# A retention layer followed by a two-layer MLP on one core: GpSimd's casts and state copies given to VectorE and ScalarE, with a new order of all work

## The chip, the cores and the metric

The kernel runs on one core of a Trainium2 chip. A core has a matrix engine (TensorE, "PE" in the profile, with its weight loads shown apart as "PEld"), three engines for elementwise work (VectorE "DVE", ScalarE "ACT", GpSimd "POOL"), and a fifth, SyncE ("SP"), which here only issues DMAs. Each engine works through its own instructions strictly in order; a DMA is issued by one engine's queue and then runs on 16 shared DMA engines. The metric is the device time of one execution in microseconds, the median of several runs.

## The reference

Inputs are q, k and v, each [8 batches, 8 heads, 576 positions, 64] in float32, and two weight matrices, w_in [512, 2048] and w_out [2048, 512]. What is computed:

```python
scores = scale * np.matmul(q, k.transpose(0, 1, 3, 2))
gamma = 1.0 - 2.0 ** (-5.0 - np.arange(H))            # one decay per head
rel = pos[:, None] - pos[None, :]
Dmat = np.where(rel >= 0, gamma[:, None, None] ** rel, 0.0)
attn = np.matmul(scores * Dmat, v)                    # [8, 8, 576, 64]
x = attn.transpose(0, 2, 1, 3).reshape(4608, 512)     # tokens x (heads * 64)
h = x @ w_in
out = np.maximum(0.01 * h, h) @ w_out                 # leaky ReLU, [4608, 512] float32
```

## The kernel before

**Attention in units.** The 4608 tokens are cut into 36 units of 128 tokens (two chunks of 64). Because the decay is a power of gamma, it is split into a factor on q and a factor on the inverse side, and the sum over earlier chunks is carried from unit to unit as a state of 64 x 64 per head. Each unit u runs these jobs; their names are the words in the order below:

- `ldU.0`, `ldU.1`, `ldU.2`: loads of q, k and v of unit U, 256 KB each (line 347). Where a unit crosses from one batch to the next (unit 4, for one), a load is two DMAs. Each of the three has four buffers in turn, so the load for unit U waits for the cast of unit U-4.
- `ckU` casts k to 16 bits (line 365); `cqU` and `cvU` cast q and v and multiply them with decay factors from a table (`scaled`, lines 367 to 373). On VectorE and GpSimd a scaled cast is one instruction over 128 x 512; on ScalarE it is eight, one for each head.
- The transposes of k and q: for the first 12 units on TensorE (`tpU.1`, `tpU.0`, line 403), each followed by a copy out of PSUM (`ytU.1`, `ytU.0`, line 410); from unit 12 on by one DMA transpose on SP's queue (`trU`, line 389).
- `sbU`: TensorE forms the new part of the state (line 446). `stU.0` and `stU.1` add it to the old state on VectorE (line 480), `sgU.j` scales it at the end of a block (line 491), and `sxU` casts it to 16 bits (line 505).
- `caU`: TensorE multiplies q with the state and forms the scores (lines 543, 437); `mkU` applies the causal mask on VectorE (line 452); `owU` multiplies the scores with v (line 543); `xU` copies the result out of PSUM into x, transposed and in 16 bits (line 592).

**The MLP in groups.** Four units make a group of 512 tokens, g = 0 to 8. For groups 0 and 1 layer 1 is done plainly: `hG.F.T` is a set of matmuls (line 639), `lG.F.T` the leaky ReLU on ScalarE (line 646). From group 2 on layer 1, and for all groups layer 2, is done as a product of 2 x 2 blocks with seven instead of eight block products (the function `seven`). Layer 1 has four such sets in each group, `aG.0` to `aG.3`, layer 2 one, `bG`. In a set the parts `p1` to `p7` are the seven products on TensorE (lines 825 and 901), `cA` copies a partial sum from one PSUM bank to another (line 764), `u2` and `k5` copy partial sums to SBUF (lines 775 and 778), and `11`, `12`, `21`, `22` are the four results. `xsG.n` (line 805), `mG.n.x` (line 877), `wsN.x` (line 714) and `wmN.x` (line 685) are sums of blocks of x, of the layer's middle values, of w_in and of w_out, all on VectorE. Four PSUM banks serve the products in turn. `soG` stores output through SP's queue (line 729).

**Weights.** `wi0` to `wi3` load w_in in four pieces of 512 columns (two DMAs each, line 615), `wo0` to `wo3` load w_out in four pieces (line 621). All go through GpSimd's queue, and turn float32 into 16 bits on their way.

**What sets the order.** Three things, all written out. `CFG["loads"]` names the queue of each load. `ENGINE` lists, for each of VectorE, ScalarE and GpSimd, the jobs that it takes; a job that is not listed goes to a default (`ck`, `x`, `sx`, `cA`, `u2`, `k5` to ScalarE; `cq`, `cv`, `yt`, `sg` to VectorE). `ORDER` is one list of all jobs, some 1,440 words; an engine's own order is that list with the other engines' jobs left out. `name@n` gives the PSUM bank, and `+6@0` means six matmuls on a zero tile, whose result nobody reads. Nothing is decided while the kernel runs: an engine that comes to a job whose inputs are not there waits, with everything behind it.

The change touches `CFG`, `ENGINE` and `ORDER`, and three lines of the code. The helper that sends a job to its engine is short:

```python
ke, qe, ve = by(f"ck{u}", "ACT"), by(f"cq{u}", "DVE"), by(f"cv{u}", "DVE")
def scaled(out, x, e):
    if e != "ACT":
        engine[e].tensor_tensor(out=out, in0=t32[u, 2 * x][:], in1=decay(u, x), op=MUL)
        return
    for h in range(H):
        nc.scalar.mul(out=out[:, h, :], in_=t32[u, 2 * x][:, h, :], mul=tab_sb[:, w, x, h : h + 1])
```

## Time and profile before

| | us |
|---|---|
| median of 3 runs | 284.77 (284.27 to 285.83) |
| the profiled execution | 285.75 |
| its span, first to last instruction | 284.0 |
| busy: TensorE, its weight loads | 271.3, 230.0 |
| busy: VectorE, ScalarE, GpSimd | 234.6, 185.8, 85.5 |

A row of the groups of instructions reads: line, engine, operation, output <- inputs, shapes and types, number, then busy time and the mean duration in ns of one, then the idle time of the engine just before them and what ended it. A row of a timeline reads: start, duration, engine, line, operation, number; a bracket tells how long the engine had been idle and what it waited for. A row of the table by stretches gives, for each stretch of the span, the busy time and number of instructions of each engine. A duration is that of one instruction from its start to its end; since the next one begins before the last has quite ended, the distance from start to start is a little less. GpSimd's busy time holds its issuing of loads (line 347, 615 and 621) beside its arithmetic.

### The profile page before, as it was taken

Reading aid. Unit: us, or ns where it says so; the run is one execution under the profiler, and the core shown is the slowest. Engines: PE = TensorE matmul, PEld = TensorE weight load, DVE = VectorE, ACT = ScalarE, POOL = GpSimd, SP = SyncE. Lnnn points to the kernel's source line nnn. Section 1 sums busy time; section 2 is a strip of 40 time slices with the busy share of each in tenths; the row PEclk is TensorE's granted clock in tenths of the full one; section 3 lists DMA queues with packets and bytes.
Section 4 is the critical chain, followed back from the end, with each engine's and each line's share of the span. In section 5 each row is a group of like instructions: output and inputs, shape, how many; then the busy total and the mean of one; then the engine's idle time right before and its main releaser. Section 6 shows DMA issues by size and latency. Waiting matters only on the chain.

```text
span 284.0 us, 10281 instructions
## 1 busy us (share of the span) xinstructions
PE 271.3 (96%) x4412; PEld 230.0 (81%) x4412; DVE 234.6 (83%) x422; ACT 185.8 (65%) x401; POOL 85.5 (30%) x103
## 2 busy tenths in 40 slices
PE   7779999989999999999999999999999999999994
PEld 3358887878888888888888887888888888888883
DVE  2873889868999998988999899999889977884761
ACT  2615756716835977789589855896698576646910
POOL 8996897846230802010011132410011000000000
PEclk9999999999999999999999999999999999999999
DMA  7999899998999799889527996797849323001104
GB/s 224 251 187 256 196 246 201 197 307 204 286 224 231 176 198 178 202 165 276 106 63 173 257 242 129 159 265 164 201 79 290 79 58 130 2 2 74 76 0 149
DMA packets 115021, 49.00 MB, mean 173 GB/s; under 512 B 103712, under 2 KB 108448, under 8 KB 114976
## 3 DMA queue, kind: packets, MB, share of 16 engines
q1 hardware_dynamic: 107632, 35.14, 53.2%
q0 software_dynamic: 7056, 13.11, 19.9%
q8 instruction: 34, 0.56, 0.9%
q10 hardware_dynamic: 288, 0.11, 0.2%
q14 instruction: 11, 0.09, 0.1%
HBM read 36.81 MB, written 9.44 MB: 163 GB/s over the span
## 4 chain that ended last, share of the span: by engine, by line
PE 70%; DMA 13%; POOL 8%; DVE 3%; issue 3%; ACT 2%; POOLq 0%; DVEq 0%; ACTq 0%
PE acc L901 33%; PE acc L825 31%; POOL t L347 5%; DMA w_out<-in_moe_w_out_dram 4%; PE ot L543 3%; DMA w_in<-in_moe_w_in_dram 3%; DMA t<-in_v_dram 3%; DMA t<-in_k_dram 2%; PE sc L446 2%; DMA t<-in_q_dram 1%; PE sc L437 1%; DVE w_mix L685 1%; ACT qk L373 1%; POOL w_in L615 1%; POOL w_out L621 1%
## 5 line engine op out<-in xcount | busy, mean ns | idle before, releaser
L901 PEld LDWEIGHTS <-gt 128*128 128x128 f16 x720 | 69.4, 98 | 9.5 <-issue 0.8
L901 PE MATMUL acc<-w_out,gt 128*128 128x256 f16 x432 | 53.4, 273 | 0.6 <-DMA w_out<-in_moe_w_out_dram 0.6
L825 PEld LDWEIGHTS <-w_in 128*128 128x128 f16 x448 | 42.7, 98 | 6.9 <-issue 1.1
L843 ACT ACTIVATE gt<-acc 128x512 f16<-128x512 f32 x56 | 33.5, 599 | 11.8 <-PE acc L825 11.3
L901 PE MATMUL acc<-w_mix,gt 128*128 128x256 f16 x288 | 36.4, 273 | 0.0
L825 PEld LDWEIGHTS <-w_sum 128*128 128x128 f16 x336 | 32.1, 98 | 4.2
L851 ACT ACTIVATE gt<-sum 128x512 f16<-128x512 f32 x56 | 33.9, 631 | 0.9 <-DVE sum L847 0.8
L825 PE MATMUL acc<-xT,w_in 128*128 128x256 f16 x224 | 32.8, 273 | 1.1 <-DVE osb L938 0.6
L825 PE MATMUL acc<-xs,w_sum 128*128 128x256 f16 x224 | 33.1, 273 | 0.0
L825 PE MATMUL acc<-xs,w_in 128*128 128x256 f16 x224 | 32.7, 273 | 0.0
L639 PE MATMUL acc<-xT,w_in 128*128 128x256 f16 (+1 forms) x320 | 30.9, 251 | 1.5 <-DMA w_in<-in_moe_w_in_dram 1.5
L369 POOL TENSOR_TENSOR v<-t,cs 128x512 f16<-128x512 f32 x14 | 15.7, 1120 | 55.3 <-PE ot L543 45.5
L901 PEld LDWEIGHTS <-mix 128*128 128x128 f16 x288 | 27.9, 98 | 3.9 <-issue 0.5
L452 DVE TENSOR_TENSOR s<-sc,cs 128x512 f16<-128x512 f32 x36 | 24.6, 683 | 5.3 <-PE sc L437 4.8
L639 PEld LDWEIGHTS <-w_in 128*128 128x128 f16 x320 | 25.5, 98 | 4.1 <-issue 1.9
L646 ACT ACTIVATE gt<-acc 128x512 f16<-128x512 f32 x32 | 18.0, 600 | 13.5 <-PE acc L639 13.5
L775 ACT COPY u<-acc 128x512 f32<-128x512 f32 x30 | 17.6, 586 | 13.5 <-PE acc L901 9.9
L764 ACT COPY acc<-acc 128x512 f32<-128x512 f32 x27 | 15.5, 573 | 13.8 <-PE acc L825 8.3
L847 DVE TENSOR_TENSOR sum<-acc,k 128x512 f32<-128x512 f32 x28 | 19.3, 688 | 5.7 <-PE acc L825 2.8
L847 DVE TENSOR_TENSOR sum<-acc,u 128x512 f32<-128x512 f32 x28 | 19.2, 686 | 3.8 <-PE acc L825 3.5
L369 POOL TENSOR_TENSOR qk<-t,cs 128x512 f16<-128x512 f32 x12 | 13.2, 1104 | 27.2 <-DMA t<-in_q_dram 19.2
L592 ACT CAST xT<-ot 128x512 f16<-128x512 f32 x25 | 14.6, 587 | 8.2 <-PE ot L543 7.5
(70 smaller groups left out, 491.1 us busy)
## 6 DMA issues: line engine op xcount, KB each, us to landing
out_dram<-osb SPq DMA_DIRECT2D x17, 512.0 KB, 4.0
t<-in_k_dram SPq DMA_DIRECT2D x22, 256.0 KB, 4.9
t<-in_q_dram SPq DMA_DIRECT2D x22, 256.0 KB, 4.3
t<-in_v_dram SPq DMA_DIRECT2D x21, 256.0 KB, 4.2
t<-in_v_dram POOLq DMA_DIRECT2D x11, 256.0 KB, 4.7
t<-in_q_dram POOLq DMA_DIRECT2D x10, 256.0 KB, 5.5
t<-in_k_dram POOLq DMA_DIRECT2D x10, 256.0 KB, 4.6
w_in<-in_moe_w_in_dram POOLq DMA_DIRECT2D x8, 256.0 KB, 7.1
```

The lines of the kernel that those rows point to most:

```text
L369: engine[e].tensor_tensor(out=out, in0=t32[u, 2 * x][:], in1=decay(u, x), op=MUL)
L452: landed[u] = nc.vector.tensor_tensor(out=s[:], in0=sc[:, :, 0], in1=mask_sb.unsqueeze(1).unsqueeze(1).to_broadcast([P, 2, NP, CH]), op=MUL,)
L592: copies[xe](out=x_of(u).rearrange("q c (j t) -> q j c t", j=2), in_=at)
L639: nc.tensor.matmul(out=a[:, n, :], lhsT=w_in16[:, c, (f0 + n) * P : (f0 + n + 1) * P], rhs=x[:, c, t0 : t0 + nt], start=(n == 0 and c == 0 ...
L646: nc.scalar.activation(out=y[:, f0 : f0 + nf, t0 : t0 + nt], in_=a[:], func=mybir.ActivationFunctionType.Lrelu)
L764: copies[ce](out=B[:], in_=A[:])
L775: op("u2", ue, lambda: copies[ue](out=u2[:], in_=B[:]), [done["6"]], [u2], [B])
L825: nc.tensor.matmul(out=r[:, f, :], lhsT=w[:, c, (2 * n + f) * P : (2 * n + f + 1) * P], rhs=rhs[:, c, :], start=fresh and c == 0 and f == ...
L843: w = op(what, "ACT", lambda: nc.scalar.activation(out=to(), in_=r[:], func=lr), after, [y], [r])
L847: what, "DVE", lambda: nc.vector.tensor_tensor(out=s[:], in0=r[:], in1=plus[:], op=ADD),
L851: f"l{g}.{n}.{what}", "ACT", lambda: nc.scalar.activation(out=to(), in_=s[:], func=lr), [j], [y],
L901: nc.tensor.matmul(out=(r[tb] if isinstance(r, tuple) else r)[:, tb, :], lhsT=lhs[n]()[:, f, tb * P : (tb + 1) * P], rhs=rhs[n][:, f, :], ...
```

## The change

GpSimd keeps only its DMA issues. Its fifty other jobs (14 `cv`, 12 `cq`, 9 `ck`, 7 `sg`, 8 `sx`) go to VectorE or ScalarE. Between VectorE and ScalarE themselves many jobs change places too, in both directions: copies out of PSUM, casts and results of layer 2. The load of v of unit 12 goes from SP's queue to GpSimd's. `ORDER` is new from the first line to the last, with nine instead of twelve places for the matmuls on a zero tile (27 of these instead of 28). A new setting `half` is 0 and changes nothing that is computed or how. The diff, cut to its core (lines of `loads`, the new and the old `ENGINE`, the beginning and the end of `ORDER`):

```diff
-        ("u", 12, "SP"), ("u", 13, "SP"), ("u", 14, "SP"), ("u", 15, "SP"), ("u", 16, "SP"), ("u", 17, "SP"),
...
+        ("u", 12, ("SP", "SP", "POOL")), ("u", 13, "SP"), ("u", 14, "SP"), ("u", 15, "SP"), ("u", 16, "SP"),
...
+        "DVE": """
+            ck0 cq1 cq0 yt1.0 cv0 cv1 yt0.0 ck2 cq2 cv2 cq3 x0 yt1.1 yt2.0 cv3 yt3.1 yt4.1 yt3.0 cv4 cq4 x3 cq5 sx4.1
+            cv5 cv6 ck7 cq6 x5 yt6.1 yt6.0 cq7 cv8 yt7.0 sx7 x7 cv9 sx8.0 cq8 yt8.0 cv10 cv11 b0.k5 cq11 sx9 yt9.1
+            yt9.0 yt10.1 yt10.0 sx10 cq14 cv12 yt11.1 cv13 x10 cv14 ck15 a2.0.u2 a2.1.u2 a2.2.k5 cq15 ck16 cv16
+            a2.3.u2 cq18 cq16 cq17 sx16 cv18 cq19 sx17.0 cv19 cq20 a3.2.k5 a3.2.u2 a3.3.u2 cv20 cq21 sx20 cv21 cv22
...
         "ACT": """
...
-            ck0 yt0.0 sx0 ck2 yt1.1 cv2 yt1.0 x0 yt3.0 x2 yt3.1 yt4.0 cv5 x4 yt5.0 x5 sx6 yt7.1 sx7 x6 sx8.0 yt8.0
...
+            yt0.1 ck1 sx0 ck3 ck4 sx1 sx2 yt2.1 x1 x2 sx3 yt4.0 ck5 yt5.1 x4 yt5.0 sx5 ck6 cv7 yt7.1 sx6 ck8 x6 ck9
...
-        "DVE": """
-            yt0.1 cq0 cv0 cq1 cv1 ck1 cv3 cq3 yt2.0 yt2.1 sx2 x1 sg3.1 sx3 cq4 x3 ck4 yt4.1 cv4 yt5.1 cq5 sx4.1 sx5
...
-        "POOL": """
-            cq2 sg1.1 sx1 ck3 ck5 ck7 cv7 cv8 cv9 sg8.0 ck9 cv10 sx9 cq9 sg10.1 cq11 cq10 cv13 ck13 cq15 cv14 sg12.1
-            ck17 cq17 sx13.1 cv16 cq18 cq16 cq21 cv19 cv21 sx19 cv24 cq25 sg24.0 sx24 sx25 cq29 cv27 cv28 sx27 cv29
-            ck29 sg28.1 sx28 ck30 ck32 cv34 cq35 sg35.0
...
-    ld0.1 ld0.0 ld1.0 ld0.2 ld1.2 ld1.1 ck0 +6@0 +1@1 +1@2 +1@3 tp0.1@0 ld2.1 yt0.1 ld2.2 cq0 ld2.0 +6@1 tp0.0@2 cv0
-    yt0.0 cq1 ld3.2 +1@3 sb0 cv1 tp1.0@0 ld3.0 ck1 st0.0 +2@1 tp1.1@3 ld3.1 st0.1 +1@2 sb1 sx0 wi1 ck2 ca0 yt1.1 mk0
-    tp2.1@1 cv2 cq2 st1.0 ow0 wi0 cv3 st1.1 yt1.0 cq3 +5@2 sb2 x0 sg1.1 tp3.0@3 tp2.0@2 st2.0 sx1 yt2.0 yt3.0 ck3
-    yt2.1 +2@0 ca1 st2.1 ld4.0 tp3.1@3 mk1 sx2 +1@0 ow1 sb3 ca2 wi2 h0.4.0@2 x1 ld4.1 mk2 h0.4.128@1 l0.4.0 st3.0
...
-    b8.p6.1 m8.3.0 b8.p5.1 m8.3.1 b8.u2 b8.p7.0 b8.k5 b8.p7.1 b8.p2.0 b8.22 b8.p4.0 b8.11x so8.11x b8.p4.1 b8.p3.0
-    b8.21 b8.p3.1 so8.1 b8.p2.1 b8.12 so8.12 b8.11y so8.11y
...
+    ld0.1 ld0.0 ld1.0 ld0.2 ld1.1 ld1.2 ck0 +6@0 +1@1 +1@2 tp0.1@3 ld2.1 yt0.1 ld2.0 cq1 cq0 +7@0 tp1.0@1 ld3.1 yt1.0
+    tp0.0@2 cv0 ld2.2 ck1 +1@3 sb0 ld3.0 st0.0 cv1 ld4.1 yt0.0 st0.1 ck2 +7@0 sb1 sx0 cq2 ld3.2 ca0 tp2.1@1 st1.0
+    tp1.1@3 ck3 tp2.0@2 mk0 wi1 st1.1 +1@0 ow0 cv2 tp3.1@0 wi0 sg1.1 sb2 cq3 st2.0 ck4 ld4.0 x0 sx1 st2.1 yt1.1 sx2
+    yt2.0 ld4.2 tp4.1@3 yt2.1 cv3 ca1 tp3.0@2 mk1 +1@1 ow1 sb3 ca2 x1 mk2 wi2 yt3.1 +2@1 ow2 st3.0 h0.4.128@1 yt4.1
+    st3.1 h0.4.0@0 sg3.1 l0.4.128 yt3.0 x2 l0.4.0 h0.4.256@3 sx3 ld5.0 ca3 l0.4.256 h0.0.256@1 mk3 ld5.1 ld5.2 cv4
...
+    b8.p6.1 b8.p2.0 b8.u2 b8.p7.0 b8.11x so8.11x b8.p7.1 b8.p2.1 b8.22 m8.3.1 b8.p4.0 b8.11y so8.11y b8.p4.1 b8.p3.0
+    b8.21 so8.1 b8.p3.1 b8.12 so8.12
...
-        z = Buf(xs_pool, [P, 4, 2, HT], F16, "xs", turn=g - CFG["plain1"])
+        z = Buf(xs_pool, [P, 4, 2, HT], F16, "xs", turn=g - CFG["plain1"] + CFG["half"])
```

More of the change, by code (lines that the diff above doesn't have):

```diff
@@ L68 @@
     turned=12,
+    half=0,
     order='1265734',
@@ L213 @@
+    a8.2.p4.0 a8.3.k5 a8.3.p7.0 a8.2.21 m8.0.0 a8.3.p3.0 l8.2.22 b8.p1.0@2,0 a8.3.22 l8.2.12 a8.3.12 l8.3.22 b8.p1.1
+    m8.1.0 l8.3.12 a8.3.p4.0 m8.0.1 b8.p5.0@3 a8.3.21 m8.2.1 b8.cA@1 b8.p5.1 m8.1.1 b8.p6.0 m8.2.0 b8.k5 m8.3.0
+    b8.p6.1 b8.p2.0 b8.u2 b8.p7.0 b8.11x so8.11x b8.p7.1 b8.p2.1 b8.22 m8.3.1 b8.p4.0 b8.11y so8.11y b8.p4.1 b8.p3.0
+    b8.21 so8.1 b8.p3.1 b8.12 so8.12
 """
@@ L985 @@
         for i in range(16):
-            layer1(g, 2 * (i % 8), 2, 2 * P * (i // 8), 2 * P)
+            if g + 1 < CFG["plain1"] or i % 4 < 2 or not CFG["half"]:
+                layer1(g, 2 * (i % 8), 2, 2 * P * (i // 8), 2 * P)
     mix_weights()
@@ L989 @@
     for g in range(NG):
-        if g >= CFG["plain1"]:
+        whole_plain = CFG["plain1"] - CFG["half"]
+        if g >= whole_plain:
             z = x_sums(g)
-            for n in range(HF // 2):
+            for n in range(HF // 4 if g < CFG["plain1"] else 0, HF // 2):
                 layer1_set(g, n, z)
```

209 lines of the change are left out of this document (101 added, 108 removed), and 7 rows, old and new, of the table loads.

## The prediction

> **What bounds the kernel now.** I read the head of the page, then a table of busy time by stretch, then TensorE's own timeline for the places where it waits, then the chain of work that ended last. First the head of the page and six stretches of the table (columns: stretch, length, then busy time and instructions of each engine, granted TensorE clock, DMA share, GB/s).
>
> ```profile
> PE 271.3 (96%) x4412; PEld 230.0 (81%) x4412; DVE 234.6 (83%) x422; ACT 185.8 (65%) x401; POOL 85.5 (30%) x103
> ...
> 0.00:20.00 20.00, 14.21 (x251) 7.79 (x252) 12.34 (x26) 7.76 (x18) 18.83 (x28) 1.00 0.94 222
> 40.00:60.00 20.00, 18.86 (x319) 16.16 (x320) 16.55 (x27) 11.89 (x23) 16.68 (x19) 1.00 1.09 209
> 80.00:100.00 20.00, 20.00 (x355) 16.99 (x353) 19.47 (x38) 13.11 (x25) 8.24 (x9) 1.00 0.96 199
> 260.00:284.00 24.00, 20.23 (x182) 17.43 (x179) 13.50 (x21) 9.60 (x19) 0.00 (x0) 1.00 0.18 67
> ...
> 137.60:188.10 50.50, 49.86 (x914) 42.79 (x913) 47.52 (x85) 39.14 (x89) 11.76 (x14) 1.00 0.72 166
> 20.00:260.00 240.00, 236.85 (x3986) 204.77 (x3984) 208.78 (x376) 168.45 (x365) 66.69 (x76) 1.00 0.78 179
> ```
>
> From 20 to 260 us TensorE is without work for 240.00 - 236.85 = 3.15 us, at a granted clock of 1.00. The rest of its idle time lies in the first 20 us (5.8) and in the last 24 (3.8). The same matmuls are to be done after the change, so between 20 and 260 us nothing can be won but these 3.15 us; a delay has no such limit. VectorE is full in places (19.47 of 20), GpSimd in the first 60 us. TensorE's timeline shows where the idle time lies (in brackets the idle time before the row, and what ended it):
>
> ```profile
> 19.15 1.95 PE L639 MATMUL acc<-xT,w_in 128*128 128x128 f16 x32 [1.46 <-DMA w_in<-in_moe_w_in_dram]
> ...
> 21.81 1.95 PE L639 MATMUL acc<-xT,w_in 128*128 128x128 f16 x32
> ...
> 43.25 0.38 PE L403 MATMUL acc<-ident,qk 128*128 128x128 f16 x4 [0.53 <-DVE qkT L410]
> ...
> 57.20 1.03 PE L901 MATMUL acc<-w_out,gt 128*128 128x256 f16 x8 [0.61 <-DMA w_out<-in_moe_w_out_dram]
> ...
> 62.83 0.38 PE L901 MATMUL acc<-w_mix,mix 128*128 128x256 f16 x2 [0.32 <-DVE w_mix L685]
> ...
> 72.23 0.22 PE L543 MATMUL ot<-qkT,st 64*64 64x64 f16 x2 [0.39 <-ACT qkT L410]
> ...
> 117.51 0.60 PE L825 MATMUL acc<-xT,w_in 128*128 128x256 f16 x4 [0.51 <-ACT acc L764]
> ...
> 172.96 0.60 PE L825 MATMUL acc<-xT,w_in 128*128 128x256 f16 x4 [0.62 <-DVE osb L938]
> ```
>
> Six waits after 20 us make 0.53+0.61+0.32+0.39+0.51+0.62 = 2.98 of the 3.15 us. The first layer-1 matmul waits for a piece of w_in. The chain that ended last says the same: GpSimd's issues and the transfers of w_in and w_out early on, TensorE at the end.
>
> ```profile
> 11.70 1.08 POOL qk L369
> ...
> 13.32 8.35 DMA w_in<-in_moe_w_in_dram
> ...
> 50.19 10.34 DMA w_out<-in_moe_w_out_dram
> ...
> 267.81 12.43 PE acc L901 x112
> ...
> 280.27 0.37 ACT osb L936
> ```
>
> The row at 267.81 gives TensorE's pace: 12.43 / 112 = 0.111 us for each matmul of 256 columns.
>
> **The change part by part.** *Work that moves.* Fifty jobs leave GpSimd: 14 cv, 12 cq, 9 ck, 7 sg, 8 sx. Several others change places between VectorE and ScalarE. Counted by the two tables of engines, VectorE gains 17 long and 14 short instructions net, ScalarE 17 single ones and two of the scaled casts that it does in eight parts. Prices, from the timelines of VectorE, ScalarE and GpSimd (start, duration):
>
> ```profile
> 6.16 0.69 DVE L369 TENSOR_TENSOR qk<-t,cs 128x512 f16<-128x512 f32 x1 [0.60 <-DMA t<-in_q_dram]
> 6.78 0.69 DVE L369 TENSOR_TENSOR v<-t,cs 128x512 f16<-128x512 f32 x1
> ...
> 8.59 0.42 DVE L365 CAST qk<-t 128x512 f16<-128x512 f32 x1
> 8.93 0.42 DVE L478 COPY s<-sc 128x256 f32<-128x256 f32 x1
> ...
> 113.20 1.27 DVE L491 TENSOR_TENSOR s<-stmp,cs 128x256 f32<-128x256 f32 x1
> ...
> 169.85 1.52 DVE L369 TENSOR_TENSOR v<-t,cs 128x512 f16<-128x512 f32 x1
> ...
> 172.23 0.68 DVE L938 TENSOR_TENSOR osb<-acc,u 128x512 f32<-128x512 f32 x1
> ```
> ```profile
> 11.36 2.02 ACT L373 ACTIVATE v<-t,cs 128x64 f16<-128x64 f32 x8
> 13.28 0.57 ACT L410 COPY qkT<-acc 128x512 f16<-128x512 f16 x1
> ```
> ```profile
> 8.43 1.05 POOL L347 DMA_DIRECT2D t<-in_q_dram  x1
> 9.48 0.88 POOL L347 DMA_DIRECT2D t<-in_k_dram  x1
> ...
> 15.92 1.61 POOL L347 DMA_DIRECT2D t<-in_q_dram  x2
> ...
> 29.62 0.61 POOL L365 CAST qk<-t 128x512 f16<-128x512 f32 x1 [2.90 <-PE acc L639]
> ...
> 113.09 1.10 POOL L369 TENSOR_TENSOR v<-t,cs 128x512 f16<-128x512 f32 x1 [0.77 <-DVE osb L938]
> ...
> 169.34 1.49 POOL L369 TENSOR_TENSOR v<-t,cs 128x512 f16<-128x512 f32 x1
> ```
>
> A long VectorE instruction follows the next after 6.78 - 6.16 = 0.62 us, a short one after 8.93 - 8.59 = 0.34. So VectorE gains 17 x 0.62 + 14 x 0.34 = 15.3 us; ScalarE 17 x 0.57 + 2 x 2.02 = 13.7 us, on 185.8, which leaves it at 70% of the span. ScalarE's part is hidden by its idle third; if a part of it stands ahead of a copy that frees a bank, TensorE pays it, and that is in the last term of the sum.
>
> *What VectorE gets back.* The scaled cast of v at 169.85 took 1.52 us while GpSimd ran another (169.34 to 170.83); alone it takes 0.69. The scaling at 113.20 took 1.27 beside GpSimd's of 113.09; as a short one I put it at 0.42. Each lost about 0.85 us. The groups of instructions, shapes apart (count, then busy us and mean ns), show how often:
>
> ```profile
> L369 DVE TENSOR_TENSOR v<-t,cs 128x512 f16<-128x512 f32 x16 | 14.0, 882 | 0.0
> L877 DVE TENSOR_TENSOR gt<-gt 128x1024 f16<-128x1024 f16 x18 | 13.9, 778 | 0.0
> ```
>
> Against 0.69 that is 16 x 0.19 + 18 x 0.09 = 4.7 us in these two groups. With GpSimd out of the arithmetic it goes, and VectorE's net gain is 15.3 - 4.7 = 10.6 us, to 245.2 (86% of the span). The waits at 117.51 and 172.96 stand right behind the two stretched instructions: at 172.96 TensorE waits for a VectorE sum that ran at 172.23, 0.85 us late; at 117.51 for a ScalarE copy behind VectorE's line. Both waits (0.51 and 0.62) are shorter than what is given back. I take -1.1 us; the bounds are 0 (something else is late there next) and -1.1.
>
> *w_out.* GpSimd's casts stood between its loads: the one at 29.62 held the queue 2.90 us for its data. Without them the loads go out earlier, but the DMA engines are full then (share 1.09 from 40 to 60 us). I take 2.9 us earlier, the one hold that left the queue empty; bounds 0 and 2.9 and more. The new order asks for the second piece of w_out (b0.p1.1) some 18 matmuls of 0.111 us, 2.0 us, sooner. Net 0.9 us, about what the waits of 0.61 and 0.32 need: -0.9, between -0.9 and +2.0.
>
> *The front.* In the new order k of unit 4, two DMAs of together 1.6 us of issue (as q of that unit at 15.92), goes ahead of the first w_in piece. That piece then comes 0.9 (one load's issue at 9.48) to 1.6 us later; I take 0.9, since the transfers and not the issues are the slower there (8.35 us to land). The scaled cast of 1.08 us between the two w_in pieces is gone, so the second comes -0.2 to +0.9 later. Before the change TensorE had two layer-1 steps on the first piece (19.15 for 1.95) and took up the second at 21.81, just after it landed (13.32 + 8.35 = 21.67). The new order has three such steps first, so it hardly waits for the second: of 0.9 us some 0.5 are made good, +0.4 (0 to +1.2). VectorE has 12 long and 17 short instructions ahead of that first step, 13.2 us from 6.16 on, so until 19.4; w_in comes at about 20.05. The cover is 0.6 us thin.
>
> *v of unit 12* moves from SP's queue to the end of GpSimd's, behind all its other loads. SP's queue starts with k of unit 12 instead; nothing waits behind GpSimd's last issue, and its cast comes some 18 us of matmuls later. Price 0; if the DMA engines hold it, the cast waits on VectorE with all behind it.
>
> *The end.* Before, TensorE's last product is followed by a 0.37 us copy and a store of 128 KB; now by the sum b8.12 and a store of 256 KB. The sum takes 0.69 us:
>
> ```profile
> 279.39 0.69 DVE L938 TENSOR_TENSOR osb<-acc,u 128x512 f32<-128x512 f32 x1 [1.06 <-PE acc L901]
> ...
> out_dram<-osb SPq DMA_DIRECT2D x17, 512.0 KB, 4.0
> out_dram<-osb SPq DMA_DIRECT2D x2, 128.0 KB, 1.7
> ```
>
> That is +0.3 for the sum, and for the store between 0 and (4.0 - 1.7) = 2.3; being twice the small one and half the large, I take a little over the small one, +0.2. Together +0.5.
>
> *New waits.* An order made anew has its own. Waits of the other kind in the old one (0.53 and 0.39) stay at their size. For the fuller VectorE and ScalarE I add 0.8 us, near the 0.92 of those two; the bounds are 0 and the 10.6 us by which VectorE grows.
>
> Sum: -1.1 - 0.9 + 0.4 + 0.5 + 0.8 = -0.3 us. The profiled execution took 285.75 us (its span 284.0), the median of the runs 284.77, 0.98 less. 285.75 - 0.3 - 0.98 = 284.4 us.
>
> **A rule weighed.** The issue at 8.43 took 1.05 us, while VectorE's cast of 8.59 ran, against 0.88 for the next: 0.17 us lost. Ahead of the first w_in piece the new order has two such casts on VectorE (k of units 0 and 2), the old one had one (unit 1): 0.17 us more, and the sum would be -0.1; I leave it in the front's bounds. The Trainium skill, "SBUF — State Buffer", sections "SBUF: two separate sides" and "A bandwidth-pool intuition that's wrong (but worth ruling out)", says that such a copy keeps GpSimd from writing its DMA descriptors, and gives some 3.1 us for an issue of 0.62. By that figure, an estimate, w_in would come 2.5 us later and the sum would be about +1.7 with the 0.5 made good. The direction agrees with the row, the size is fifteen times the row's, and the row decides.
>
> **The rivals.** *Slower: VectorE becomes the bound in the middle.* From a4.0.p1 to a6.0.p1 both orders have 392 matmuls; VectorE has 60 long instructions in both, and 25 short ones before, 32 after. In 50.50 us it was busy 47.52. The seven add 2.4 us, to 49.9; freedom from GpSimd's 14 jobs there gives back 0 to 14 x 0.85, at least the 0.85 of 169.85. With nothing else back, VectorE is at 49.1 of 50.5, and half its idle time of 3.0 us must go. Against: from 80 to 100 us it was busy 19.47 of 20, and TensorE did not wait. It decides when VectorE waits for data or for a product over 1.4 us in that stretch; if it waits the 3.0 as before, TensorE is 1.6 us late there, and twice that over the like stretches before and after. In place of 0.8: -0.3 - 0.8 + 3.2 + 1.2 (the front at its upper end, 0.8 more, and 0.4 for w_out) = +3.3, so 288.1 us.
>
> *Faster: the new order has no waits of its own.* Then all of the 3.15 us goes, and only the end is left: -3.15 + 0.4 + 0.5 = -2.25, 282.5 us; with the front made good too, 282.1. For it: load leads are longer (casts of units 9 to 11 come 9 to 18 us of matmuls behind their loads, 7 to 14 before). Against: fuller engines.
>
> *TensorE has room.* Its weight loads were busy 81%, and 16.99 of 20 us where matmuls had no gap at all, so 85% is full here; at 85% for the whole, 230.0 / 0.85 = 271 us. The matmul pace of 0.111 us without gaps speaks against it. The Trainium skill, "Perfetto Trace Analysis", section "Identifying the Most-Contended Engine", holds weight-load busy time to be the measure of room, and matmul busy time not.
>
> *Slower: casts hold the loads.* The one early cast more on VectorE stops GpSimd's issues for longer than the 0.17 us seen. To bring the sum from -0.3 to +1.7 it must cost 2.0 us; the time is then 284.77 + 1.7 = 286.5. The issues at 8.43 and 9.48, 1.05 and 0.88, with and without such a cast beside them, speak against it.
>
> **How the numbers follow.** Half a per cent, 1.4 us, is about what a measurement can tell from no change: 283.35 to 286.2. Forecast 0.39; VectorE bound 0.29; casts that hold the loads 0.03; no waits of its own 0.27; room on TensorE 0.02. So faster 0.29, same 0.39, slower 0.32. The forecast's own range, from the bounds of the front, the end and w_out, is 283.4 to 286.2. The range goes to 281.6, half a microsecond below the faster rival, and 288.2, the slower rival.
>
> **What would show it.** Scaled casts on VectorE at 0.69 us with no GpSimd arithmetic in the groups; no wait for w_out near 57 us; the first layer-1 matmul at about 20 us; no wait like those at 117.51 and 172.96; b8.12 last. The prediction is wrong if VectorE's line in the middle shows gaps and TensorE waits for its sums, or if ScalarE stands long before a cast (k of unit 28, on ScalarE, comes only some 4.5 us of matmuls behind its load).

## The result and the profile after

The changed kernel takes 283.32 us (median of 20 executions, 282.45 to 285.72). The kernel before, run beside it, takes 285.61 us (20 executions, 284.27 to 289.16). The ratio is 0.9927, with an interval of 0.9907 to 0.9947: it is faster by 0.7%. The 284.77 us that the prediction started from is the median of three of these twenty executions of the kernel before; that of all twenty is 0.84 us higher.

The profiled execution of the changed kernel was the slowest of its twenty, 285.72 us. So a second profile of the same kernel was taken later, of an execution of 283.01 us (median there 283.31). Both are shown; the second is the typical one. In the changed kernel the line numbers are lower by three (901 became 898, 825 became 822, 639 became 636, 369 became 366).

The head of the page and the summary of the chain that ended last, then rows of the table by stretches, first profile:

```profile
PE 273.8 (96%) x4411; PEld 232.3 (82%) x4411; DVE 237.9 (84%) x453; ACT 198.2 (70%) x434; POOL 40.9 (14%) x54
...
PE 92%; DMA 4%; POOL 2%; DVE 1%; issue 0%; POOLq 0%
...
20.00:260.00 240.00, 239.89 (x4040) 207.23 (x4032) 213.84 (x408) 180.12 (x401) 24.60 (x30) 0.99 0.78 177
138.30:188.30 50.00, 50.00 (x902) 43.02 (x899) 48.21 (x95) 39.55 (x88) 0.00 (x0) 1.00 0.87 182
```

GpSimd does nothing behind its last load issue, VectorE and ScalarE have more to do (213.84 and 180.12 us between 20 and 260, against 208.78 and 168.45 before), and TensorE's idle time in these 240 us went from 3.15 us to 0.11 (its matmuls ran at half clock in the first six of them, of which more below). In the stretch of the sets a4 to a6 (138.30 to 188.30) VectorE is busy 48.21 of 50.00 us and TensorE 50.00 of 50.00: the engine that feeds it is nearly full, and it is never late. TensorE's timeline has no row with a wait between 30 and 280 us. What there is lies in the first 30:

```profile
16.38 0.58 PE L400 MATMUL acc<-ident,qk 128*128 128x128 f16 x4 [2.21 <-DVE qkT L407]
19.52 0.43 PE L540 MATMUL ot<-s,v 64*64 64x64 f16 x16 [1.12 <-DVE s L449]
21.95 4.66 PE L636 MATMUL acc<-xT,w_in 128*128 128x128 f16 x48
...
278.23 1.91 PE L898 MATMUL acc<-w_out,gt 128*128 128x256 f16 x16
```

The same kernel's second profile, table by stretches and TensorE's timeline:

```profile
20.00:260.00 240.00, 239.32 (x4017) 206.87 (x4018) 214.71 (x409) 181.62 (x404) 23.90 (x28) 1.00 0.78 180
...
16.12 0.58 PE L400 MATMUL acc<-ident,qk 128*128 128x128 f16 x4 [2.21 <-DVE qkT L407]
20.26 1.96 PE L636 MATMUL acc<-xT,w_in 128*128 128x128 f16 x32
...
275.52 1.91 PE L898 MATMUL acc<-w_out,gt 128*128 128x256 f16 x16
```

Three points of time cut each execution into front, middle and end: the first layer-1 matmul, the end of the last matmul (start plus duration of its row; before: 277.45 + 2.78), and the end of the span. For the two profiles after, the last three columns are differences to before.

| | first layer-1 matmul | end of last matmul | end of span | front | middle | end |
|---|---|---|---|---|---|---|
| before | 19.15 | 280.23 | 284.0 | 19.15 | 261.08 | 3.8 |
| after, first profile | 21.95 | 280.14 | 283.9 | +2.80 | -2.89 | under 0.1 |
| after, second profile | 20.26 | 277.43 | 281.2 | +1.11 | -3.91 | under 0.1 |

So the new kernel starts layer 1 about 1 us later, has a middle nearly 4 us shorter, and ends as before. About 0.5 us of both is work that moved, not time lost and won. Ahead of its first layer-1 matmul the new order has a set of four transposes (k of unit 4) and the 24 matmuls of `ow2` more than the old one. Rows of TensorE's timeline, second profile, then before:

```profile
19.95 0.32 PE L540 MATMUL ot<-s,v 64*64 64x64 f16 x16
20.09 0.23 PE L540 MATMUL ot<-qkT,st 64*64 64x64 f16 x8
```
```profile
21.03 0.32 PE L543 MATMUL ot<-s,v 64*64 64x64 f16 x16
```

From 19.95 to the layer-1 matmul at 20.26 `ow2` takes 0.31 us; before, it comes behind the first layer-1 matmul, at 21.03. The four transposes add some 0.22 (eight of them last 0.62 us in the profile of before, four 0.40). At equal work the second profile therefore loses 1.11 - 0.53 = 0.58 us in front and wins 3.91 - 0.53 = 3.38 us in the middle.

Why the first profile lost more in front can be read from its rows. The chain has the load of v of unit 3; VectorE's timeline has its cast, which stands ahead of the mask of unit 1 (line 449) that TensorE is waiting for:

```profile
10.62 7.53 DMA t<-in_v_dram
...
15.91 0.75 DVE L407 COPY qkT<-acc 128x512 f16<-128x512 f16 x2
18.17 0.69 DVE L366 TENSOR_TENSOR v<-t,cs 128x512 f16<-128x512 f32 x1 [1.51 <-DMA t<-in_v_dram]
18.78 0.68 DVE L449 TENSOR_TENSOR s<-sc,cs 128x512 f16<-128x512 f32 x1
```

The load landed at 10.62 + 7.53 = 18.15 us. In the second profile the same cast ran at 16.32 us without a wait. TensorE was then idle a second time, and its granted clock stayed low; table by stretches (PE alone; the column behind its busy time is the clock), first and second profile:

```profile
18.00:20.00 2.00, 0.88 (x38) 0.50 1.24 213
20.00:22.00 2.00, 2.00 (x71) 0.50 1.07 282
22.00:24.00 2.00, 2.00 (x24) 0.50 1.08 193
```
```profile
16.00:18.00 2.00, 1.88 (x33) 0.50 1.14 165
18.00:20.00 2.00, 1.86 (x72) 0.66 1.22 217
20.00:22.00 2.00, 2.00 (x55) 1.00 1.12 296
```

The Trainium skill, "TensorE: Matmul & The Clock Gate", section "Part 1: The HAM clock gate (the "warmup" mystery)", puts the clock at half after an idle window of some 3.4 us. The half agrees (0.50); an idle time of 2.21 us, behind a stretch with shorter gaps, was enough here.

### The profile page after: what moved, and what is told of

It reads as the page before. It is cut to its first block, busy times and chain, and to the rows that moved or that the text cites. A ratio compares the mean times of both kernels' runs of the same rounds, so it can differ in the third digit from the quotient of the medians.

```text
span 283.9 us, 10247 instructions
## 1 busy us (share of the span) xinstructions
PE 273.8 (96%) x4411; PEld 232.3 (82%) x4411; DVE 237.9 (84%) x453; ACT 198.2 (70%) x434; POOL 40.9 (14%) x54
## 4 chain that ended last, share of the span: by engine, by line
PE 92%; DMA 4%; POOL 2%; DVE 1%; issue 0%; POOLq 0%
PE acc L898 40%; PE acc L822 31%; PE acc L636 11%; PE ot L540 5%; DMA t<-in_v_dram 4%; PE sc L443 2%; PE sc L434 2%; POOL t L344 2%; PE acc L400 1%; PE acc L957 0%; DVE osb L935 0%; DVE v L366 0%; DVE s L449 0%; POOLq L344 0%; POOLq L1009 0%
## 5 line engine op out<-in xcount | busy, mean ns | idle before, releaser
L898 PE MATMUL acc<-w_out,gt 128*128 128x256 f16 x432 | 54.4, 273 | 0.0
L822 PEld LDWEIGHTS <-w_in 128*128 128x128 f16 x448 | 43.1, 98 | 5.7 <-issue 0.3
L840 ACT ACTIVATE gt<-acc 128x512 f16<-128x512 f32 x56 | 33.4, 599 | 10.8 <-PE acc L822 10.6
L636 PE MATMUL acc<-xT,w_in 128*128 128x256 f16 (+1 forms) x320 | 32.2, 262 | 0.0
L636 PEld LDWEIGHTS <-w_in 128*128 128x128 f16 x320 | 27.1, 104 | 2.5 <-DVE xT L589 0.2
L761 ACT COPY acc<-acc 128x512 f32<-128x512 f32 x32 | 18.4, 574 | 13.3 <-PE acc L822 9.1
L772 ACT COPY u<-acc 128x512 f32<-128x512 f32 x26 | 15.3, 589 | 8.9 <-PE acc L898 4.5
L366 DVE TENSOR_TENSOR qk<-t,cs 128x512 f16<-128x512 f32 x29 | 19.8, 685 | 1.9 <-DMA t<-in_q_dram 1.9
L366 DVE TENSOR_TENSOR v<-t,cs 128x512 f16<-128x512 f32 x29 | 19.7, 685 | 1.6 <-DMA t<-in_v_dram 1.5
L589 ACT CAST xT<-ot 128x512 f16<-128x512 f32 x28 | 16.3, 588 | 6.7 <-PE ot L540 6.4
```

Source lines behind the costliest of these rows:

```text
L589: copies[xe](out=x_of(u).rearrange("q c (j t) -> q j c t", j=2), in_=at)
L636: nc.tensor.matmul(out=a[:, n, :], lhsT=w_in16[:, c, (f0 + n) * P : (f0 + n + 1) * P], rhs=x[:, c, t0 : t0 + nt], start=(n == 0 and c == 0 ...
L761: copies[ce](out=B[:], in_=A[:])
L772: op("u2", ue, lambda: copies[ue](out=u2[:], in_=B[:]), [done["6"]], [u2], [B])
L822: nc.tensor.matmul(out=r[:, f, :], lhsT=w[:, c, (2 * n + f) * P : (2 * n + f + 1) * P], rhs=rhs[:, c, :], start=fresh and c == 0 and f == ...
L840: w = op(what, "ACT", lambda: nc.scalar.activation(out=to(), in_=r[:], func=lr), after, [y], [r])
```

## The experiments

The prediction gave two reasons for a gain (GpSimd's arithmetic no longer stretches VectorE's; w_out comes earlier) and feared two losses (new waits, a later front). The experiments ask which part of the change does what. All ratios are against the kernel before, run in the same batch.

| run | ratio | 95% interval |
|---|---|---|
| the change | 0.9927 | 0.9907 to 0.9947 |
| the change, second time | 0.9927 | 0.9903 to 0.9951 |
| old order, three casts off GpSimd | 1.0003 | 0.9970 to 1.0036 |
| old order, twelve early jobs off GpSimd | 1.0049 | 1.0013 to 1.0086 |
| old order, all fifty jobs off GpSimd | 1.0269 | 1.0227 to 1.0311 |
| old order, whole new table of engines | 1.0696 | 1.0634 to 1.0758 |
| new order, late 33 jobs back on GpSimd | 0.9922 | 0.9889 to 0.9954 |
| new order, all fifty back on GpSimd | 1.0213 | 1.0136 to 1.0290 |
| new, nine short jobs more on VectorE | 1.0010 | 0.9975 to 1.0045 |
| new, w_in ahead of k of unit 4 | 1.0151 | 1.0126 to 1.0177 |
| new, another front | 0.9901 | 0.9875 to 0.9928 |
| new, another front, old end | 0.9902 | 0.9868 to 0.9936 |
| new, another front, late 33 back on GpSimd | 0.9905 | 0.9867 to 0.9942 |

### The old order with three casts off GpSimd

```diff
         "DVE": """
+            cv19 cv27 cv28
...
         "POOL": """
-            ... cv19 ... cv27 cv28 ...
```

> The old kernel with only three casts of v (units 19, 27 and 28) taken from GpSimd to VectorE, at their old places in the order. In the trace of before each of them ran beside a VectorE instruction that took 1.3 to 1.5 us instead of 0.42 to 0.69. Theory (collision): the TensorE waits of 0.51 us at 117.5 and 0.62 us at 173.0 go, although VectorE gets 3 x 0.62 = 1.9 us more work; the time falls by 1.1 to 1.5 us, ratio about 0.995. Rival (VectorE is simply full there): the waits stay or move, ratio 1.000 to 1.005.

Measured: ratio 1.0003. TensorE's timeline and the table by stretches of this run (lines are higher by one than before):

```profile
172.03 0.60 PE L826 MATMUL acc<-xT,w_in 128*128 128x256 f16 x4 [0.56 <-DVE osb L939]
...
100.00:120.00 20.00, 20.00 (x344) 17.27 (x342) 19.34 (x40) 15.10 (x38) 1.04 (x1) 1.00 1.04 203
```

The wait at 117.51 is gone, so there the collision was its cause, or at least enough to cause it. The wait at 172 stays, though GpSimd's cast is gone: VectorE's sum is late there anyway (VectorE is busy 19.78 of 20 us from 160 to 180 in this run). By the waits about half of the -1.1 us in the prediction was right. In time nothing of it shows: the theory's 0.995 missed, and an interval of 0.3% (0.9 us) to either side can't tell half a microsecond from none.

### The new order with the late jobs back on GpSimd

Units 12 and up: 33 jobs (the expectation says 34).

```diff
         (the same jobs go out of "DVE" and "ACT")
+        "POOL": """
+            cv13 ck13 cq15 cv14 sg12.1 ck17 cq17 sx13.1 cv16 cq18 cq16 cq21 cv19 cv21 sx19 cv24 cq25 sg24.0 sx24
+            sx25 cq29 cv27 cv28 sx27 cv29 ck29 sg28.1 sx28 ck30 ck32 cv34 cq35 sg35.0
+        """,
```

> The new kernel and its new order, but with the jobs of units 12 to 35 that GpSimd had before (34 of the 50) given back to it. It is the table alone, undone for the part behind the loads. Theory (collision): VectorE and ScalarE are less full, but VectorE's scaled casts and scalings beside GpSimd's stretch to over 1 us again, and TensorE has waits of 0.5 us and more between 60 and 240 us, 1 to 3 us in sum; ratio to the old kernel 0.996 to 1.003. Rival (the new order made the gain, and where the casts run does not matter): no more waits than in the new kernel (0.1 us), ratio 0.993.

Measured: ratio 0.9922, no different from the change. The table by stretches:

```profile
20.00:260.00 240.00, 239.66 (x4020) 207.07 (x4020) 207.45 (x387) 173.97 (x375) 55.45 (x61) 1.00 0.81 180
```

GpSimd works 55.45 us beside VectorE, and TensorE idles 0.34 us. VectorE is stretched now and then here too (a sum of 128 x 1024 of 1.10 us at 160.30, 0.93 at 168.41, instead of 0.69), but nothing waits for it at that time. Behind the loads, then, it isn't GpSimd's silence that makes TensorE's line free of waits.

### The new order with all fifty jobs back on GpSimd

This differs from the run above by the 17 jobs of units 1 to 11. The exchange of other jobs between VectorE and ScalarE stays as in the changed kernel. (The new order with the whole old table was not run, so what that exchange is worth in the new order stays open.)

> The new order and the new loads, with all fifty jobs put back on GpSimd, the twelve early ones among its load issues too. Theory (the order alone carries the gain behind the loads): between 80 and 260 us TensorE idles under 0.5 us as in the changed kernel; if the early jobs cost the loads nothing either, the ratio to before is 0.990 to 0.995. By the rival that the freed GpSimd queue is what brings w_out early, w_out lands 5 us or more later than in the changed kernel, a wait of 0.5 us or more for it stands near 50 us, the two casts of q of unit 2 and k of unit 3 hold w_in by 1 to 2 us, and the ratio is 0.997 to 1.005.

Measured: ratio 1.0213. The profiled execution, 294.30 us, is the slowest of its four (the others: 289.48 to 292.77), so the sizes below are those of one execution. Both ratios expected miss. The theory's first half holds: behind 80 us TensorE is as full as in the changed kernel (busy 20.00 us in eight of the nine stretches of 20 us from 80 to 260, and 19.97 in the other), so the loss lies ahead of that. The rival's cause is not there: w_in and w_out aren't what TensorE waits for. The timelines of VectorE, GpSimd and TensorE around the largest wait, and the table by stretches:

```profile
58.70 3.18 DVE L877 TENSOR_TENSOR gt<-gt,mix 128x1024 f16<-128x1024 f16 x1
...
59.27 1.06 POOL L369 TENSOR_TENSOR qk<-t,cs 128x512 f16<-128x512 f32 x1
60.27 1.05 POOL L369 TENSOR_TENSOR v<-t,cs 128x512 f16<-128x512 f32 x1
61.27 2.95 POOL L369 TENSOR_TENSOR qk<-t,cs 128x512 f16<-128x512 f32 x2
61.80 1.52 DVE L685 TENSOR_TENSOR w_mix<-w_out 128x1024 f16<-128x1024 f16 x1
...
63.25 1.53 DVE L877 TENSOR_TENSOR mix<-mix,gt 128x1024 f16<-128x1024 f16 x1
65.03 0.68 DVE L369 TENSOR_TENSOR qk<-t,cs 128x512 f16<-128x512 f32 x1
...
65.77 0.61 PE L403 MATMUL acc<-ident,qk 128*128 128x128 f16 x4 [3.82 <-DVE qk L369]
...
60.00:80.00 20.00, 16.18 (x170) 13.47 (x169) 16.36 (x25) 6.87 (x17) 5.96 (x7) 0.83 0.48 115
```

Four scaled casts on GpSimd, nearly back to back since its queue had been held (4.13 us, for a product of VectorE, up to 55.58), meet three sums on VectorE, which take 3.18, 1.52 and 1.53 us in place of 0.68. That is 4.2 us on VectorE's line, and the cast behind them (65.03) is what TensorE waits 3.82 us for. With the wait the granted clock falls too: 0.83 in the mean from 60 to 80 us. Here GpSimd's arithmetic is the cause, at many times the 0.85 us of the prediction. The rest of the loss lies in the first 60 us: waits that the changed kernel doesn't have, of 1.18 us at 12.99, 0.72 at 34.09, 0.65 at 43.37 and 0.38 at 50.55 (all but the second for VectorE), and a granted clock of 0.50 from 14 to 22 us.

### The old order with the twelve early jobs off GpSimd

```diff
         "DVE": """
+            cq2 sg1.1 sx1 ck3 ck5 ck7 cv7 cv8 cv9 sg8.0 ck9 cv10
```

> The kernel before with its twelve early GpSimd jobs (casts and copies of units 1 to 10, which stand among the issues of w_in, w_out and units 5 to 11) on VectorE; all else as before. By the prediction's step for w_out the waits of 0.61 (57.20 us) and 0.32 (62.83 us) go, for -0.9 us, less what VectorE's eight long and four short instructions cost the first 20 us (0 to 1 us): ratio 0.997 to 1.000. By the rival that VectorE pays at the front, as the changed kernel did, the first layer-1 matmul comes 1 to 3 us later than 19.15 and the ratio is 1.000 to 1.010.

Measured: ratio 1.0049. The first layer-1 matmul comes at 18.32 us, 0.83 earlier than before, and the waits of 0.61 and 0.32 us at 57 and 63 us are gone, as the prediction's step for w_out says. (The wait of 0.61 is not a sure sign: the run with three casts, whose first 60 us are those of the kernel before, doesn't have it either, though its last piece of w_out is issued at 49.94 us.) TensorE's timeline shows where it is lost again (lines higher by one than before):

```profile
76.08 2.06 PE L902 MATMUL acc<-w_mix,mix 128*128 128x256 f16 x16 [1.34 <-DVE mix L878]
...
173.38 0.60 PE L826 MATMUL acc<-xT,w_in 128*128 128x256 f16 x4 [1.42 <-DVE osb L939]
```

VectorE, with more ahead of a product's sum, is late for it at 76 us, and the wait at 173 is 1.42 us where it was 0.62. The rival put the loss in front; it came behind, so the rival's ratio, 1.000 to 1.010, was met by another way than it said.

### The old order with the whole new table, and with the fifty jobs alone

The first run takes the new `ENGINE` whole, the second moves only the fifty GpSimd jobs (34 to VectorE, 16 to ScalarE) and leaves the other 117 that the new table places elsewhere. `ORDER` and the loads are the old ones in both.

> The old order of issue and the old loads, with the new table of engines: GpSimd does no cast or copy any more. By the theory that the gain comes from taking arithmetic off GpSimd, the waits at 57.20, 117.51 and 172.96 us of the kernel before go and the time falls by 1 to 2 us (ratio 0.993 to 0.997). By the theory that the order made anew carries the gain, an order that was made for another table has waits of its own: TensorE idles at least the 3.15 us of before between 20 and 260 us, and the time is no lower than before, up to 3 us above (ratio 1.000 to 1.010).

> The kernel before, its order and loads unchanged, with only the fifty GpSimd jobs moved: 34 to VectorE and 16 to ScalarE, as in the new table; the other 117 jobs that the new table places elsewhere (between VectorE and ScalarE) stay where they were. If the old order's loss with the whole new table (16.9 us at TensorE's last matmul) came from those 117 jobs, this kernel is near the one before, ratio 0.997 to 1.010. If taking the work off GpSimd is what the old order cannot bear, because VectorE and ScalarE are asked for more between two products than fits, it loses most of it too: ratio 1.02 to 1.06, with TensorE waiting for VectorE and ScalarE all along the middle.

Measured: 1.0696 and 1.0269. The first is far above both of its expected ranges; the second lies in that of its second theory. Table by stretches and summary of the chain, for the whole table and then for the fifty jobs:

```profile
20.00:260.00 240.00, 225.99 (x3833) 191.66 (x3830) 201.18 (x384) 172.39 (x389) 24.13 (x29) 1.00 0.78 176
...
PE 53%; ACT 20%; DVE 15%; issue 5%; DMA 4%; SPq 1%; POOL 0%; ACTq 0%; DVEq 0%; POOLq 0%
```
```profile
20.00:260.00 240.00, 233.14 (x3924) 200.38 (x3922) 210.31 (x402) 178.47 (x413) 25.05 (x30) 0.99 0.78 177
...
PE 76%; DMA 7%; ACT 7%; DVE 6%; issue 2%; POOL 2%; SPq 0%; ACTq 0%; POOLq 0%
...
74.64 0.22 PE L545 MATMUL ot<-qkT,st 64*64 64x64 f16 x2 [1.32 <-ACT qkT L412]
...
218.87 0.60 PE L827 MATMUL acc<-xs,w_sum 128*128 128x256 f16 x4 [1.65 <-ACT u L777]
```

ScalarE's timeline ahead of that last wait, again with the fifty jobs alone:

```profile
215.85 2.02 ACT L375 ACTIVATE v<-t,cs 128x64 f16<-128x64 f32 x8
217.77 0.57 ACT L938 COPY osb<-acc 128x512 f32<-128x512 f32 x1
218.24 0.58 ACT L777 COPY u<-acc 128x512 f32<-128x512 f32 x1
```

VectorE and ScalarE do no more between 20 and 260 us than in the changed kernel (210.31 and 178.47 against 213.84 and 180.12), and yet TensorE waits 6.9 us in the one and 0.11 in the other. What differs, where the rows show it, is which job stands ahead of which: the cast of a v that came from GpSimd, 2.02 us in its eight parts, now stands on ScalarE ahead of the copy that TensorE waits for (218.24), since the order has it there. In the old order, taking the work off GpSimd is a loss of 2.7%, and the other moves of the table cost 4% more.

### More work on VectorE

```diff
         "DVE": """
+            ck21 ck22 sx19 ck23 sx21 sx23 ck25 ck26 ck28
...
         "ACT": """
-            (the same nine)
```

> The changed kernel with nine short jobs of units 19 to 28 (casts of k of units 21, 22, 23, 25, 26 and 28, state copies of units 19, 21 and 23) moved from ScalarE to VectorE: 9 x 0.34 = 3.1 us more on VectorE between 133 and 170 us, where it has 50.00 - 48.21 = 1.8 us idle in 50. By the rival that VectorE is at its limit in the middle, TensorE pays what does not fit, 3.1 - 1.3 = 1.8 us or more, in waits ended by VectorE, and the time rises by 1.5 to 3 us (ratio to before 0.998 to 1.004). By the theory that the work ahead of each product has slack in it, waits stay under 0.5 us and the ratio is that of the changed kernel, 0.990 to 0.995.

Measured: ratio 1.0010, where the changed kernel has 0.9927; in spans, 282.8 against the 281.2 of the second profile, +1.6 us. The stretch that holds the nine jobs, in this run and in the second profile of the changed kernel:

```profile
130.00:170.00 40.00, 39.06 (x691) 33.15 (x689) 39.35 (x81) 25.37 (x52) 0.00 (x0) 1.00 0.80 177
...
137.21 1.05 PE L899 MATMUL acc<-w_out,gt 128*128 128x256 f16 x8 [0.78 <-DVE gt L875]
```
```profile
130.00:170.00 40.00, 40.00 (x705) 34.40 (x702) 38.66 (x76) 31.00 (x64) 0.00 (x0) 1.00 0.85 181
```

VectorE goes from 38.66 to 39.35 of 40 us, and TensorE from full to 39.06. Of 3.1 us put on VectorE 1.6 to 2.1 come out at the end, as the rival said (1.8): VectorE is near its limit in the middle, with about 1 us of room in 40. The run can't tell, though, how much of this is VectorE's fullness and how much the places of the nine jobs, in an order that was made for them on ScalarE.

### The front

The first of two runs moves the load of k of unit 4 behind w_in. The second has the copies `yt1.1` and `x0` on ScalarE, ahead of the cast of k of unit 4, and the cast of v of unit 3 behind the mask of unit 1.

```diff
-    ... ld3.0 st0.0 cv1 ld4.1 yt0.0 ... sg1.1 sb2 cq3 st2.0 ck4 ld4.0 ...
+    ... ld3.0 st0.0 cv1 yt0.0 ... sg1.1 sb2 cq3 st2.0 ld4.1 ck4 ld4.0 ...
```
```diff
-    ... cq3 st2.0 ck4 ld4.0 x0 sx1 st2.1 yt1.1 sx2 ... yt2.1 cv3 ca1 tp3.0@2 mk1 +1@1 ow1 sb3 ca2 ...
+    ... yt1.1 x0 cq3 st2.0 ck4 ld4.0 sx1 st2.1 sx2 ... yt2.1 ca1 tp3.0@2 mk1 cv3 +1@1 ow1 ca2 sb3 ...
```

> The new kernel with one load moved: k of unit 4 (two DMAs) is issued behind the first two pieces of w_in instead of ahead of them. It undoes the step that I priced at +0.9 us of lateness and +0.4 us of time. Theory (the load ahead of w_in makes the front late): the first w_in piece is issued at 10.1 instead of 11.5 us and lands a microsecond earlier, the cast of v of unit 3 comes earlier too, and the time falls by 0.4 to 2 us; ratio 0.986 to 0.991. Rival (the front is held by VectorE's and ScalarE's lines, where the cast of k of unit 4 now comes later and holds the state casts sx1 and sx2 on ScalarE): no change or 1 us longer, ratio 0.993 to 0.997.

> The new kernel with its front loosened: the copy yt1.1 and the output copy x0 go from VectorE to ScalarE and stand before the cast of k of unit 4; on VectorE the cast of v of unit 3 stands behind the mask of unit 1 instead of before it; the state products of unit 3 stand behind the scores of unit 2. In the new kernel TensorE waited 2.2 us at 16.4 and 1.1 us at 19.5, its clock fell to about half from 14 to 27 us, and the first layer-1 step began at 21.95. Theory (VectorE's line and the late v of unit 3 hold the front): the first step begins at about 20.5, the clock stays near full, 1.5 to 3 us less than the new kernel; ratio to the old one 0.982 to 0.988. Rival (w_in's landing at 20.4 alone sets the front): the first step comes at 20.4 at the low clock, no more than 0.5 us less, ratio 0.991 to 0.993.

Measured: 1.0151 and 0.9901. With w_in first, TensorE's timeline has

```profile
22.47 0.61 PE L401 MATMUL acc<-ident,qk 128*128 128x128 f16 x4 [8.37 <-ACT qk L363]
```

ScalarE stands at the cast of k of unit 4, whose load now comes late, with the state copies of units 1 and 2 behind it; the rival named this, but allowed it 1 us. So the early load of k isn't what costs the front: the order needs it there. With the other front the wait of 2.21 us shrinks to 0.34 and the first layer-1 matmul comes at 19.80 us:

```profile
14.65 0.40 PE L402 MATMUL acc<-ident,qk 128*128 128x128 f16 x4 [0.34 <-ACT qk L364]
...
19.80 2.12 PE L638 MATMUL acc<-xT,w_in 128*128 128x128 f16 x32
```

That is 0.46 us earlier than in the second profile of the changed kernel. The medians are 282.96 and 283.31, and the intervals overlap: a small gain at most, of the rival's size. These sizes change from execution to execution: in the two later runs with this front the wait is 1.62 and 0.67 us, and the first layer-1 matmul comes at 19.60 and 20.14. The wait of 2.21 us for a copy on VectorE came from the places of copies and casts; with this front TensorE waits there for a cast of k on ScalarE instead.

### The second profile, and two attempts at a better kernel

The first of these is the changed kernel itself; the second adds to the other front the old end of the order, the third the late 33 jobs on GpSimd.

> The changed kernel once more, for a second profile of it. Theory (in its first profile v of unit 3 landed late by chance, at 18.15 us, and TensorE stood idle long enough that its clock was granted at half): this time v lands near 16 us, the front costs 0.7 to 0.9 us against the kernel before at equal work of TensorE and not 3.9, and the span is 281 to 282. Rival (the front of this order always costs this much): first layer-1 matmul at 21.9 us again and a span near 284. The ratio is 0.990 to 0.995 either way.

> The changed kernel with the new front of the earlier run (copies of units 0 and 1 on ScalarE ahead of the cast of k of unit 4) and with the end of the order as it was before the change: the product of b8.p2.1 last, then the narrow copy and the 128 KB store. By the prediction's step for the end (+0.5 for a 0.69 us sum and a 256 KB store behind the last product) the time falls by 0.3 to 0.5 us against the run with the new front alone, to a ratio of about 0.988, and the time from TensorE's last matmul to the end of the span is 0.3 us or more shorter. By the rival that the end costs nothing, since from TensorE's equal work to the end of the span both kernels took 3.9 us, the ratio is that of the run with the new front, 0.990.

> The changed kernel with the new front and, besides, the 33 jobs of units 12 and up back on GpSimd: both edits that were tried alone. If VectorE at its limit still costs the changed kernel something in the middle (small idle times of TensorE that no wait shows), relieving it adds to the new front and the ratio falls to 0.986 to 0.988. If TensorE is full from 20 to 260 us already, the two edits together give no more than the new front alone, 0.989 to 0.992.

Measured: 0.9927, 0.9902 and 0.9905. The second profile did what the theory said: the cast of v at 16.32 us, the front 0.58 us longer at equal work (0.7 to 0.9 expected), the span 281.2. The old end brings nothing in time; its profile has a shorter tail (TensorE's last matmul ends at 277.63, the span at 280.87: 3.2 us), but a wait of 0.67 us for a ScalarE copy ahead of it (270.36), since the new table gives the copies of the last group to ScalarE. GpSimd's help on top of the other front brings nothing either, as TensorE has no idle time left to win. The three kernels with the other front have medians of 282.96, 282.81 and 282.57 us; among them, and against the change by itself, nothing can be told apart.

## Why the prediction was right or wrong

**The sum.** Forecast: -0.3 us on a median of 284.77, so 284.4, no measurable change the likeliest. Measured: 283.32, inside the range and on the faster side, -2.3 us against the kernel before beside it. Against the 284.77 us that the forecast started from it is -1.45. What came is the rival "the new order has no waits of its own": it said -2.25 us with the front at +0.4. Its mechanism was right, but that its number fits so well is in part luck: its middle of -3.15 gave -3.4, its front of +0.4 gave 0.6, and its end of +0.5 gave nothing, so between the two profiles the sum is -2.8. Its chance, 0.27, was too low. The step of the forecast that failed is its middle: -1.1 - 0.9 + 0.8 = -1.2 us where -3.4 came, with new waits added and two old ones kept that were not there.

**New waits (+0.8 taken, 0 to 10.6).** They measured next to nothing: TensorE waits 0.11 us (first profile) and 0.68 (second, 0.58 of it ahead of 26 us) between 20 and 260 us, and the old order's waits of 0.53 and 0.39, which I had kept, went too. I took the waits of the old order as the measure of what any order must have. But an order made for its table can place each job by when it is needed. VectorE's growth was real (208.78 to 213.84 us in these 240) but smaller than I had it, and the runs with the old order show what it costs where the order doesn't fit: 2.7 and 7.0%.

**Collisions (-1.1 taken).** The two waits are gone, and VectorE's scaled casts are no longer stretched (29 of v at a mean of 685 ns, row below, where 16 had 882). What VectorE got back was more than I counted: its busy time grew by 3.3 us (234.6 to 237.9), not by 10.6, so some 12 us came back and not 4.7. I had looked at two groups; in the trace of before 16 of VectorE's two-input instructions last longer than the usual 0.42 or 0.68 us, by 10.3 us together, and none in the changed kernel. But as a reason for the time it was half wrong. Taking three casts off GpSimd in the old order removed one wait of the two, and putting 33 jobs back in the new order brought none. Ahead of 80 us, on the other hand, the collisions would have cost the new order much more than I allowed.

**w_out (-0.9 taken).** Right in direction, and the lead is larger. Rows of GpSimd's timeline and of VectorE's groups in the first profile:

```profile
37.34 0.94 POOL L344 DMA_DIRECT2D t<-in_v_dram  x1
...
40.77 0.81 POOL L618 DMA_DIRECT2D w_out<-in_moe_w_out_dram  x1
...
L366 DVE TENSOR_TENSOR v<-t,cs 128x512 f16<-128x512 f32 x29 | 19.7, 685 | 1.6 <-DMA t<-in_v_dram 1.5
```

The last piece is issued at 40.77 us (first profile) and 38.70 (second), where the chain of before had it at 50.19: 9.4 and 11.5 us earlier, not 2.9. No row of TensorE waits for it, and the waits at 57.20 and 62.83 are gone. Either part of the change brings most of this lead: with the twelve early jobs off GpSimd in the old order the last piece is issued at about 41 us, and in the new order with all fifty jobs back on GpSimd at 43.38. What it is worth in time isn't shown, since the wait at 57.20 comes and goes in the old order.

**The front (+0.4 taken, 0 to +1.2).** By the first layer-1 matmul it is +1.11 in the second profile and +2.80 in the first; at equal work the second, typical one is 0.58, near what I took. (The first layer-1 matmul moves by some tenths from profile to profile: 18.77 us in the run with three casts, whose front is that of before; 19.68 and 20.47 in the runs with nine short jobs and with the late 33, whose front is that of the changed kernel.) But the way there was wrong. I looked for the first piece of w_in; when the layer-1 matmul began, w_in had landed, and TensorE had stood 2.21 us for a copy on VectorE (L407) and then run at half its clock. "The cover is 0.6 us thin" named the right engine and priced it at nothing.

**The end (+0.5 taken).** Between the kernels it measured nothing: from the last matmul to the end of the span 3.8 us before and 3.8 in both profiles after. But this time isn't steady with the old end: over the six runs' profiles that have it, 3.2 to 4.2 us; over the eight with the new end, 3.8 to 3.9. So the runs show no cost of the wider sum and the larger store, and can't exclude one of this size.

**What idle time costs.** The old middle had 3.15 us of idle time in sight, and the new one, with 0.68, is 3.91 us shorter. The rows show a part of the difference: a set of four matmuls lasts 0.60 us but the next begins 0.43 later,

```profile
250.25 0.60 PE L822 MATMUL acc<-xT,w_in 128*128 128x256 f16 x4
250.68 1.04 PE L898 MATMUL acc<-w_out,gt 128*128 128x256 f16 x8
```

so 0.17 us of each wait is counted as busy. For the six waits that is 1.0 us, and some 0.7 when the two of the second profile (0.27 and 0.31 us, ahead of 26 us) are taken off; with 3.15 - 0.68 = 2.5 and the 0.5 of moved work that is 3.7 of the 3.9. My "nothing can be won but these 3.15 us" was therefore too low a bound by about a third.

**The rivals.** *VectorE becomes the bound in the middle*: it didn't, but it is close; it was put at 49.1 of 50.5 us and measured 48.21 of 50.00, and with nine short jobs more TensorE waits for it. The rival's point of decision, half of VectorE's idle time used up, was about right: 1.34 of 40 us are harmless, and with 0.65 of 40 TensorE is late. *Casts hold the loads*: not seen; GpSimd's issues of one load take 0.88 to 1.04 us in the first profile (37.34, above, is one), and those between its first and the first piece of w_in 0.88 or 0.89, where before one took 1.05 beside a cast and 0.88 without. The figure of the Trainium skill's "SBUF — State Buffer" (section "A bandwidth-pool intuition that's wrong (but worth ruling out)"), some 3.1 us, doesn't agree with the trace. *TensorE has room*: no; its matmuls have no gap behind 30 us, and weight loads stay at 82% of the span.

## What to carry to other kernels

Where an order of work and a division of work among engines are both written out, they have to be made for each other: here the new division in the old order cost 2.7 to 7%, the new order with the fifty jobs back on GpSimd 2.1%, and the two together gained 0.7%. Not every job counts alike: with 33 of the fifty back on GpSimd, all behind the loads, the new order was as fast. So price such a change by what the two do together, by whether the engine that feeds TensorE still fits in its stretch (48.21 of 50 did, some 3 us more in 40 did not), and not by the waits of the old order. When a wait goes, count the pipeline's overlap lost at it (0.17 us here) beside the idle time in sight.

## What the runs showed of the hardware

TensorE's granted clock fell to 0.50 within an idle time of 2.21 us, at 15.5 us in the first profile and at 15.9 in the second, by the traces' clock records (a trace notes each change of the granted clock). In the second profile it was back at 1.00 after 3.41 us; in the first a second idle time of 1.12 us came while it was low, and it stayed low for 10.24 us, three times as long. In all runs here a stretch at half clock that ends inside the span lasts 3.41, 6.83 or 10.24 us. Even where no wait from 9 to 17 us was longer than 0.42 us (the other front) it fell, at 16.8 us, with TensorE busy 1.35 us from 14 to 16 and 1.56 from 16 to 18:

```profile
18.00:20.00 2.00, 2.00 (x65) 0.50 1.16 182
```

The kernel before was busy 1.56, 1.32 and 0.85 us in the three stretches from 14 to 20, and its profiled execution was granted 1.00 in its first 20 us. So neither the longest gap nor the busy share of these stretches alone decides it; what does isn't settled here. It has its price: 18 of the 20 executions of the changed kernel have a mean granted clock of 0.982 to 0.994, and the two with 1.00 are its fastest, 282.45 and 282.53 us.

A VectorE sum of 128 x 1024 elements took 3.18 us in place of 0.68 while GpSimd ran scaled casts back to back (59.27, 60.27, 61.27): one VectorE instruction was held over at least two of GpSimd's, so the two didn't take turns. In the prediction's rows one collision had cost 0.85 us.
